# Five plain column pairs instead of six in the first pass, and the second pass's weight sums in its pairs of columns

## The chip, the cores and the metric

The kernel runs on one core of a Trainium2 chip. The metric is the device time of one execution in microseconds (us). TensorE (PE) multiplies matrices, VectorE (DVE), ScalarE (ACT) and GpSimd (POOL) do the element-wise work, SyncE (SP) issues the transfers (DMA). Each engine runs its instructions in the order in which the program has them, and waits on semaphores for the others.

## The reference, cut to what matters

```python
scores = scale * q @ k.T                      # 8 batches, 8 heads, 576 positions, 64 wide
ret = (scores * Dmat) @ v                     # Dmat: gamma ** (i - j) for j <= i, 0 above
x = ret.transpose(0, 2, 1, 3).reshape(4608, 512)
h = x @ w_in                                  # 512 x 2048
g = maximum(h, 0) + log1p(exp(-abs(h)))       # softplus
out = g @ w_out                               # 2048 x 512, float32
```

## The kernel before

Attention has no softmax, so it is done in chunks: within a chunk scores, mask and values, between chunks a state per head. Its output, transposed, is x. The 4608 tokens are 9 units of 512; the two layers then are products of 128x128 weight blocks with 512 tokens. Every float32 operand is split in a high and a low part, and a product of blocks is the three products low x high, high x low and high x high: each is a matmul of 128x128 by 128x512, and a product over two 128-row tiles is 6 of them (`product`). For the second layer `second` does 6 for one block.

Unit 0 opens the kernel alone, while the weights are split. Then units are taken two by two. With two units and two rows and columns of blocks a product needs 8 block products, or 7 in Strassen's (Winograd's) form, with sums of the blocks of weights and of tokens as operands: B11, B21, T1, T2, B22, T3, NT4 name the token sides in the order of use.

- **First pass** (units 1 and 2): the columns of w_in are 8 pairs J. The first `PLAIN` pairs go plain: `plain_slot` is called for 2 x PLAIN columns of unit 1, each with two products, then for as many of unit 2. The other pairs go through `strassen_pair`, 7 products for both units between the two stretches; unit 2's hidden values of these are kept in DRAM and used after its own slots (`kept_parts`). The second layer of these units is plain (`output_some`).
- **Second pass on**: three times `full_pair` for J = 0 to 7 and then `full_phase`, with both layers in the seven-product form.

The weights' sums are made while the first pass runs. `prepare*` makes those of w_in for pair j (4 subtractions or additions on DVE after a sum of the high and low parts, then a split: ACT makes the high part, DVE the low), and stores them as `combined{j}`. `whole_out`, `combine_out`, `split_out` and `store_out` (or `queue_store`) do the same for w_out, as `outcombined{j}`. Before, sums 0 to 4 of w_out are made in the first pass, and 5, 6 and 7 in the first eight `full_pair`s of the second pass, by the table `job(at, ...)`, whose number is the pair J in whose `last_difference` a step stands; `last_difference` runs as `rest[2]` of the next pair.

A ring of 7 buffers feeds the weight blocks: each `product` or `second` takes one, and issues the load of the block seven products later (`block_load`). It then issues one entry of the list `queued`, or two when more than seven are there. All loads and stores go through SP, in program order.

Attention goes on beside this, in groups of some 64 small matmuls: `chunk_products` writes scores and values to the PSUM tiles `two` and `third`. DVE then reads `two` with line 244 (`scores_out`) and line 430 (`halves_out`), and `third` for the states. In a `full_pair` with a group the order on PE is: ..., NT4, the group, the `second` of this pair, then the next pair's B11 (into `acc`) and B21 (into `two[:, 0]`), so B21 has to wait until lines 244 and 430 have read. On DVE, `rest[2:]` and with it the jobs stand in the program ahead of the group's `scores_out`.

Of the kernel before, what the change touches and what calls it, by code (L numbers as in the profile page):

```python
# [52 lines left out]
HI, LO = 0, 1  # L53
TERMS = ((LO, HI), (HI, LO), (HI, HI))
NSUPER = (NUNIT - 1) // 2
PLAIN = 6
RING = 7
QUADS = 9
B11, B22, B21, T1, T3, T2, NT4 = range(7)
# [25 lines left out]
def retention_softplus_ffn(ctx: ExitStack, tc, first, whole, others, consts, w, out):  # L85
# [440 lines left out]
    def output_out(u, tt, last=0):  # L526

        y = ys[u][tt]
        if u not in places:
            places[u] = [quad() for _ in range(2)]  # L530
        osb = places[u][tt // 2][:, tt % 2]
        if tt % 2 == last:
            nc.scalar.copy(osb, y)
        else:
            nc.vector.tensor_copy(osb, y)
        r = u * T + tt * P
        if u < 2:
            nc.sync.dma_start(out[r:r + P, :], osb)
        else:
            behind.append(lambda: nc.sync.dma_start(out[r:r + P, :], osb))  # L540

# [405 lines left out]
    def prepare_sums(j):  # L947
        combine(raws[j])
# [12 lines left out]

    def raw_store(j):
        for p, n in ((2 * j, 2 * P), (2 * j + 1, 4 * P)):
            nc.sync.dma_start(wout_dram[p][:, :, 0:n].bitcast(F32), wouts[p][:, :, 0:n].bitcast(F32))

    def whole_in(j, at):
        whole_out(j, [wout_pools[p].tile([P, 2, T], F32, tag=f"w{p}", name="sums") for p in (2 * at, 2 * at + 1)])
# [23 lines left out]
    def schedule(*rows):  # L991
        plan = {}
        for p, f, *args in rows:
            plan.setdefault(p, []).append(lambda f=f, args=args: f(*args))
        return plan

    def half_b22(i):
# [13 lines left out]
        *[(5 + 2 * j, raw_store, j) for j in range(4)])  # L1011
    starts = schedule(*[(3 + 2 * i, start_combined, i) for i in range(CPU)])
    for p in range(2 * PLAIN):
        group = groups.pop() if p % 2 == 0 and p < 10 else None
        plain_slot(1, p, B11, B21, rest, group, (), *(x.get(p, ()) for x in (jobs, starts)))

    def fetch(J):
# [1 line left out]
        nc.sync.dma_start(g, kept_dram[J])  # L1019
        return g  # L1020

    def strassen_pair(s, J, group, rest, last=False, extra=None):

        u1, u2 = 1 + 2 * s, 2 + 2 * s
        for f in rest[:1]:
# [39 lines left out]
        nc.scalar.copy(c[3], acc)  # L1065
        if extra is not None:
            combine_head(raws["out", extra])
        ab4 = softplus_of(c[3])
        queued_some(len(queued))
        if group:  # L1070
            chunk_products(*group, None)
            coming_steps = next_steps(group[0]) if s == 0 and J == NJ - 1 else []
            group_out(*group)
            if extra is not None:
                combine_rest(raws["out", extra])
            for k in coming_steps:
# [15 lines left out]
    stores = [5]  # L1092
# [7 lines left out]
    extras = {(0, NJ - 2): 1, (0, NJ - 1): 2}  # L1100
    for s in range(FULL):
        u2 = 2 + 2 * s
        first = PLAIN if s == 0 else 0
        more = s + 1 < NSUPER
        for J in range(first, NJ):
            rest, kept = strassen_pair(s, J, groups.pop() if groups else None, rest, s == 0 and J == NJ - 1,
                                       extras.get((s, J)))
        for f in rest:
            f()
        rest = []  # L1110
# [7 lines left out]
        if first:  # L1118
            blocks = schedule((0, prepare_ring, 0))
            plan = schedule(  # L1120
                *[(2 * j - 1, prepare_ring, j) for j in range(1, 4)], *[(2 * j, prepare_sums, j) for j in range(4)],
                *[(2 * j + 1, prepare_split, j) for j in range(4)], *[(2 * j + 2, prepare_store, j) for j in range(4)],
                *[(8 + 2 * i, finish_combined, i, nc.vector) for i in range(2)],
                (9, half_x, B21, STAGE[1, 0], whole, nc.vector), *[(2 * j - 7, raw_store, j) for j in range(4, NJ)],
                (4, whole_in, 3, 0), (6, combine_out, 3), (7, split_out, 3), (8, store_out, 3),
                (8, whole_in, 4, 1), (9, combine_out, 4), (10, split_out, 4), (11, store_out, 4))
            starts = schedule(*[(min(6 + 2 * i, 2 * first - 1), start_combined, i) for i in range(CPU)])
            for p in range(2 * first):
                group = groups.pop() if p % 2 else None
                if p == 0:  # L1130
                    while stores:
                        prepare_rest(stores[0])
                        prepare_store(stores.pop(0))
# [3 lines left out]
                rest = []  # L1137
            job((0, 0), finish_combined, 2, nc.vector)
            job((0, 1), half_x, B11, STAGE[0, 0], whole, nc.vector)
            job((1, 0), finish_combined, 3, nc.vector)  # L1140
            job((1, 1), half_x, B22, STAGE[1, 1], whole, nc.vector)
        else:
            for i in range(CPU):
                job((i + 1, 0), finish_combined, i, nc.vector)
            for n, (b, st) in enumerate(((B11, (0, 0)), (B21, (1, 0)), (B22, (1, 1)))):
                job((5 + n, 0), half_x, b, STAGE[st], whole, nc.vector)
        kept += [fetch(J) for J in range(first + len(kept), first + 2)]
        for n, J in enumerate(range(first, NJ)):
# [2 lines left out]
            kept_parts(u2, J, kept[n], 0)  # L1151
            for f in jobs.get((n, 0), ()):
                f()
            while stores:
                prepare_rest(stores[0])
                prepare_store(stores.pop(0))
# [190 lines left out]
    for s in range(FULL, NSUPER):  # L1347
# [90 lines left out]
```

## Time and profile before

| | us |
|---|---|
| median of 3 runs | 820.41 (820.3 to 820.49) |
| the profiled execution | 820.36 |
| its span on the core | 818.6 |
| TensorE busy | 810.1 |
| VectorE busy | 572.4 |
| ScalarE busy | 394.7 |
| GpSimd busy | 135.4 |

The profile is one execution; the span runs from its first to its last instruction, and 1.76 us of the execution's time lie around it. Busy times are sums over an engine's instructions; engines overlap, so they don't add up to the span.

### The profile page before, as it was taken

To read this page: it belongs to the slowest core of one execution; us is meant where nothing else is said; L and a number is where in the kernel's file an instruction comes from. 1 tells how busy PE (TensorE), PEld (TensorE's weight loads), DVE (VectorE), ACT (ScalarE), POOL (GpSimd) and SP (SyncE) were. 2 spreads that over 40 slices of the span, in tenths; PEclk is the share of its full clock that TensorE was granted. 3 is DMA by queue.
4 is the path that set the end of the run, shared out by engine and by line. 5 is a ranking of instruction groups with operands and counts; after the bars stand their busy time and mean duration, and the time that the engine had idled before them with its cause. 6 is when DMAs were issued, how large, how long until landed. Compare 5 with 4: busy or idle time off the path is not lost.

```text
span 818.6 us, 18782 instructions
## 1 busy us (share of the span) xinstructions
PE 810.1 (99%) x7369; PEld 664.9 (81%) x7369; DVE 572.4 (70%) x962; ACT 394.7 (48%) x698; POOL 135.4 (17%) x208
## 2 busy tenths in 40 slices
PE   8999999999999999999999999999999999999998
PEld 6778878888888888888888888888888888888886
DVE  5999976776676784756869984656769944345785
ACT  6778763324522434534354564334355644434543
POOL 4322221541121453112111000111100000000000
PEclk9999999999999999999999999999999999999999
DMA  9998879887889985698888778778757676666665
GB/s 360 322 314 288 314 241 370 292 293 254 283 307 346 329 281 171 200 318 261 276 260 298 219 222 253 255 234 262 221 170 222 216 242 199 194 195 192 201 212 172
DMA packets 149399, 209.92 MB, mean 256 GB/s; under 512 B 10816, under 2 KB 115008, under 8 KB 149312
## 3 DMA queue, kind: packets, MB, share of 16 engines
q1 hardware_dynamic: 149312, 208.72, 77.4%
q8 instruction: 59, 0.97, 0.5%
q14 instruction: 28, 0.23, 0.1%
HBM read 166.74 MB, written 41.94 MB: 255 GB/s over the span
## 4 chain that ended last, share of the span: by engine, by line
PE 97%; DMA 1%; DVE 0%; SPq 0%; issue 0%; ACT 0%; DVEq 0%
PE acc L891 21%; PE sum L1183 20%; PE y L504 16%; PE third L891 12%; PE h L465 5%; PE two L891 5%; PE two L1183 4%; PE third L226 2%; PE third L1183 2%; PE acc L1183 2%; PE two L210 2%; PE two L288 2%; PE two L300 1%; DMA raw<-whole 1%; PE bank L210 0%
## 5 line engine op out<-in xcount | busy, mean ns | idle before, releaser
L891 PE MATMUL acc<-xt,ring 128*128 128x512 f32 x768 | 193.3, 389 | 0.1
L1183 PE MATMUL sum<-parts,ring 128*128 128x512 f32 (+1 forms) x723 | 173.7, 391 | 0.0
L891 PEld LDWEIGHTS acc<-xt,ring 128*128 128x128 f32 x768 | 143.9, 188 | 30.8 <-DVE quad L1056 0.5
L1183 PEld LDWEIGHTS sum<-parts,ring 128*128 128x128 f32 x723 | 134.2, 188 | 28.2
L1177 DVE TENSOR_TENSOR parts<-g,parts 128x512 fp32r<-128x512 f32 x168 | 113.5, 692 | 52.8 <-ACT parts L1173 51.7
L504 PE MATMUL y<-wout,g 128*128 128x512 f32 x576 | 141.0, 393 | 0.0
L1173 ACT CAST parts<-g 128x512 fp32r<-128x512 f32 x168 | 103.8, 622 | 68.5 <-PE sum L1183 25.3
L504 PEld LDWEIGHTS y<-wout,g 128*128 128x128 f32 x576 | 106.6, 188 | 24.2 <-DVE g L497 1.7
L891 PE MATMUL third<-xt,ring 128*128 128x512 f32 x444 | 110.9, 389 | 0.0
L891 PEld LDWEIGHTS third<-xt,ring 128*128 128x128 f32 x444 | 83.4, 188 | 17.3
L488 ACT ACTIVATE g<-g 128x512 f32<-128x512 f32 x96 | 59.0, 631 | 78.4 <-DVE g L1205 36.2
L203 POOL TENSOR_TENSOR qv<-qv,consts_sb 128x256 f32<-128x256 f32 x61 | 43.0, 705 | 132.8 <-DMA qv<-others 129.3
L1205 DVE TENSOR_TENSOR g<-two,g 128x512 f32<-128x512 f32 x24 | 16.6, 692 | 54.2 <-PE two L891 51.8
L497 DVE TENSOR_TENSOR g<-ab,g 128x512 fp32r<-128x512 f32 x44 | 31.6, 718 | 27.4 <-ACT g L493 26.7
L465 PE MATMUL h<-xt,win 128*128 128x512 f32 x192 | 47.8, 397 | 1.5 <-ACT xt L414 1.5
L493 ACT CAST g<-ab 128x512 fp32r<-128x512 f32 x44 | 27.3, 621 | 44.5 <-PE y L504 40.6
L1203 ACT COPY g<-acc 128x512 f32<-128x512 f32 x24 | 14.1, 588 | 68.7 <-PE acc L891 68.7
L465 PEld LDWEIGHTS h<-xt,win 128*128 128x128 f32 x192 | 35.1, 188 | 10.0 <-ACT xt L414 2.2
L891 PE MATMUL two<-xt,ring 128*128 128x512 f32 x168 | 42.6, 390 | 0.0
L284 POOL TENSOR_TENSOR s<-s,consts_sb 128x256 f32<-128x256 f32 (+1 forms) x31 | 20.7, 667 | 106.7 <-DVE s L282 95.7
L891 PEld LDWEIGHTS two<-xt,ring 128*128 128x128 f32 x168 | 31.4, 188 | 6.8 <-DVE xs L430 0.3
L226 PEld LDWEIGHTS third<-qv,keys 64*64 64x64 f32 x776 | 27.0, 134 | 9.0 <-issue 8.6
(186 smaller groups left out, 1199.7 us busy)
## 6 DMA issues: line engine op xcount, KB each, us to landing
ring<-split SPq DMA_DIRECT2D x126, 256.0 KB, 4.5
ring<-combined SPq DMA_DIRECT2D x104, 256.0 KB, 3.6
ring<-outcombined SPq DMA_DIRECT2D x96, 256.0 KB, 3.4
qv<-others SPq DMA_DIRECT2D x61, 320.0 KB, 4.7
ring<-outsplit SPq DMA_DIRECT2D x72, 256.0 KB, 3.5
wst<-w SPq DMA_DIRECT2D x32, 512.0 KB, 5.8
keys<-others SPq DMA_DIRECT2D x61, 256.0 KB, 4.9
split<-win SPq DMA_DIRECT2D x16, 512.0 KB, 6.0
```

The costliest lines, as they stand in the source:

```text
L203: nc.gpsimd.tensor_mul(v, v, f.unsqueeze(2).broadcast_to([P, 4, D]))
L226: return nc.tensor.matmul(L["T"][rows[h], t, part[s]], L["kp"][rows[t], s, rows[h]], L["v"][rows[t], s, rows[h]], start=True, stop=True, s ...
L284: nc.gpsimd.tensor_mul(s, s, f.unsqueeze(2).broadcast_to([P, 2 * n, D]))
L465: nc.tensor.matmul(h, wins[p][:, a, kt * P:(kt + 1) * P], xt[:, b, T1 + kt // 2, kt % 2], start=(n == 0), stop=(n == 3 * NKT - 1))
L488: nc.scalar.activation(out, h, AF.Softplus)
L493: nc.scalar.copy(g[:, HI], ab)
L497: nc.vector.tensor_sub(g[:, LO], ab, g[:, HI].bitcast(F32))
L504: nc.tensor.matmul(ys[u][tt], g[:, a, tt * P:(tt + 1) * P], wouts[p][:, b], start=(p == 0 and n == 0), stop=(p == NF - 1 and n == 2))
L891: nc.tensor.matmul(bank, w[:, ta, kt * P:(kt + 1) * P], xt[:, tb, x, kt], start=start and k == 0, stop=k == 5, skip_group_check=True)
L1173: nc.scalar.copy(t[:, HI], g_slot(J, n))
L1177: nc.vector.tensor_sub(t[:, LO], g_slot(J, n), t[:, HI].bitcast(F32))
L1183: nc.tensor.matmul(bank[m][:, at], w[:, a, m * P:(m + 1) * P], t[:, b, at], start=start and n == 0, stop=n == 2, skip_group_check=True)
```

## The change

`PLAIN` goes from 6 to 5, so pair 5 of the first pass is a seven-product pair as 6 and 7 are. What the twelfth and eleventh slots did moves: an attention group goes from unit 2's slots to a third `strassen_pair`; the sums of w_in for pair 7 (5, 6 and 7 are needed first now, each before its pair) are made from loads of `split` inside pair 5 by `late_sums`, and sum 4 is made in unit 2's slots, from the ring; the sums 3 and 4 of w_out leave unit 2's slots, and the second pass makes 3, 7, 4, 5 and 6 in that order. `ring_sum`s stand two in a slot instead of four. The stores of units 0 and 1 of the output and those of `raw_store` go through `queued` instead of straight to SP.

```diff
-PLAIN = 6
+PLAIN = 5
...
-        if u < 2:
-            nc.sync.dma_start(out[r:r + P, :], osb)
-        else:
-            behind.append(lambda: nc.sync.dma_start(out[r:r + P, :], osb))
+        (queued if u < 2 else behind).append(lambda: nc.sync.dma_start(out[r:r + P, :], osb))
...
-            nc.sync.dma_start(wout_dram[p][:, :, 0:n].bitcast(F32), wouts[p][:, :, 0:n].bitcast(F32))
+            queued.append(lambda p=p, n=n: nc.sync.dma_start(wout_dram[p][:, :, 0:n].bitcast(F32),
+                                                             wouts[p][:, :, 0:n].bitcast(F32)))
...
-        (6, prepare_ring, 4, 0, 3, 2), (7, prepare_store, PLAIN + 1), (7, prepare_ring, 4, 3, 4, 3),
-        (7, finish_combined, 1, nc.vector), (7, half_b22, 2), (8, prepare_sums, 4), (9, prepare_ring, 5),
-        (9, finish_combined, 2, nc.vector), (10, prepare_split, 4), (10, prepare_sums, 5), (10, half_b22, 3),
-        (11, prepare_store, 4), (11, finish_combined, 3, nc.vector), (11, prepare_head, 5),
+        (7, prepare_store, PLAIN + 1), (7, finish_combined, 1, nc.vector), (7, half_b22, 2), (8, prepare, PLAIN + 2),
+        (9, finish_combined, 2, nc.vector), (9, half_b22, 3), (9, finish_combined, 3, nc.vector),
...
-        for j in stores:
-            prepare_rest(j)
+        if more is not None:
+            prepare_whole(more)
+            prepare_sums(more)
...
+            if more is not None:
+                prepare_rest(more)
+                stores.append(more)
...
-                *[(2 * j - 1, prepare_ring, j) for j in range(1, 4)], *[(2 * j, prepare_sums, j) for j in range(4)],
...
-                (4, whole_in, 3, 0), (6, combine_out, 3), (7, split_out, 3), (8, store_out, 3),
-                (8, whole_in, 4, 1), (9, combine_out, 4), (10, split_out, 4), (11, store_out, 4))
...
+                *[(2 * j - 1, prepare_ring, j, 0, 2) for j in range(1, first)],
+                *[(2 * j, prepare_ring, j, 2, 4) for j in range(1, first)],
...
         if s == FULL:
-            rest = [lambda: None, lambda: None, lambda: whole_in(5, 4), lambda: combine_out(5)]
-            for at, f, *args in ((0, split_out, 5), (0, queue_store, 5), (1, whole_out, 6), (2, combine_out, 6),
-                                 (3, split_out, 6), (3, queue_store, 6),
-                                 (3, lambda: whole_out(7, spare[:2])), (4, combine_out, 7), (5, split_out, 7),
-                                 (5, queue_store, 7)):
-                job(at, f, *args)
+            homes = ((7, lambda: whole_out(7, spare[:2])), (4, lambda: whole_in(4, 7)), (5, lambda: whole_out(5)),
+                     (6, lambda: whole_out(6, spare[:2])))
+            rest = [lambda: None, lambda: None, lambda: whole_out(3), lambda: combine_out(3)]
+            j = 3
+            for at, (following, take) in enumerate(homes):
+                job(at, split_out, j)
+                job(at, queue_store, j)
+                job(at, take)
+                job(at, combine_out, following)
+                j = following
+            job(len(homes), split_out, j)
+            job(len(homes), queue_store, j)
```

Where the second pass's sums stand on DVE is seen in pair 1 of the first eight `full_pair`s. Lines 1274 and 1275 (before) and 1273 and 1274 (changed) are `last_difference`; 673 and 670 are the split's low parts, 652 and 649 `whole_out`, 659 to 662 `combine_out`; 244 and 430 read the attention group's `two`. Before:

```order
L1274 TENSOR_TENSOR g1_4132<-g1_4132 128x512
L1275 TENSOR_TENSOR g1_4132<-g1_4132,g0_4131 128x512 [waits DVE_49]
L673 TENSOR_TENSOR sums_4232<-sums_4232 128x512 [waits Activation_49]
L673 TENSOR_TENSOR sums_4233<-sums_4233 128x512 [waits Activation_49]
L244 TENSOR_TENSOR a_4495<-two_1736,mask_106 128x512 [waits PE_49]
L430 TENSOR_TENSOR xs_595<-two_1736,consts_sb_105 128x4x128
L280 COPY s_4500<-third_1738 128x256 [waits PE_49,Pool_49]
```

With the change, in the same pair:

```order
L1273 TENSOR_TENSOR g1_4109<-g1_4109 128x512
L1274 TENSOR_TENSOR g1_4109<-g1_4109,g0_4108 128x512 [waits DVE_49]
L670 TENSOR_TENSOR quad_4209<-quad_4209 128x512 [waits Activation_49]
L670 TENSOR_TENSOR quad_4210<-quad_4210 128x512 [waits Activation_49]
L649 TENSOR_TENSOR quad_4198<-wout14_979 128x512 [waits DMAHW7_49]
L649 TENSOR_TENSOR quad_4199<-wout15_980 128x512
L659 TENSOR_TENSOR quad_4198<-quad_4198,quad_4199 128x256 [waits DVE_49]
L660 TENSOR_TENSOR quad_4198<-quad_4198 128x256 [waits DVE_49]
L661 TENSOR_TENSOR quad_4199<-quad_4199,quad_4198 128x256 [waits DVE_49]
L662 TENSOR_TENSOR quad_4199<-quad_4198 128x256
L244 TENSOR_TENSOR a_4478<-two_1736,mask_106 128x512 [waits PE_49]
L430 TENSOR_TENSOR xs_595<-two_1736,consts_sb_105 128x4x128
```

Two split operations stood ahead of line 244; now two of the split, two of the next sum's `whole_out` and four of its `combine_out` do. Pairs 2, 3 and 4 have the same eight, for the sums 7 and 4, 4 and 5, 5 and 6. On PE the changed kernel has at the end of pair 1 and the start of pair 2 (the last matmuls of the group, `second`, B11, B21, T2):

```order
L226 MATMUL third_1738<-qv_4328,keys_4339 64x64
L1182 MATMUL sum_4202<-parts_4196,ring_4337 128x512 [waits DMAHW4_49,PE_49,Activation_49]
L1182 MATMUL sum_4202<-parts_4196,ring_4337 128x512 [waits DVE_49]
L1182 MATMUL sum_4202<-parts_4196,ring_4337 128x512
L1182 MATMUL sum_4203<-parts_4196,ring_4337 128x512 x3
L888 MATMUL acc_1737<-xt_186,ring_4348 128x512 [waits DMAHW6_49,Activation_49]
L888 MATMUL acc_1737<-xt_186,ring_4348 128x512 x5
L888 MATMUL two_1736<-xt_186,ring_4364 128x512 [waits DMAHW7_49,DVE_49]
L888 MATMUL two_1736<-xt_186,ring_4364 128x512 x5
L888 MATMUL acc_1737<-xt_186,ring_4374 128x512 [waits DMAHW1_49,Activation_49]
```

This order is the same in both kernels; the matmul into `two` waits for DVE, and what moved is what DVE has to do first. On SP, at the turn from the first seven-product pair of the first pass to the second, the loads for the attention groups stand among the ring's loads. Before (pairs 6 and 7; `keys` and `qv` are the attention's inputs):

```order
L162 DMA keys_2803<-others 128x512 [waits DMAHW1_49,PE_49]
L623 DMA ring_2818<-split0_107 128x2x256 [waits DMAHW2_49,PE_49]
L168 DMA qv_2820<-others 128x640 [waits DMAHW3_49,Pool_49]
L623 DMA ring_2829<-split0_107 128x2x256 [waits DMAHW4_49,PE_49]
L168 DMA qv_2831<-others 128x640 [waits DMAHW5_49,Pool_49]
L623 DMA ring_2853<-split1_108 128x2x256 [waits DMAHW6_49,PE_49]
L162 DMA keys_2855<-others 128x512 [waits DMAHW7_49]
```

With the change, at pairs 5 (the first of three) and 6:

```order
L162 DMA keys_2705<-others 128x512 [waits DMAHW1_49,PE_49]
L620 DMA ring_2720<-split14_121 128x2x256 [waits DMAHW2_49,PE_49]
L168 DMA qv_2722<-others 128x640 [waits DMAHW3_49,Pool_49]
L620 DMA ring_2731<-split14_121 128x2x256 [waits DMAHW4_49,PE_49]
L168 DMA qv_2733<-others 128x640 [waits DMAHW5_49,Pool_49]
L678 DMA combined7_0_137<-quad_2494 128x1024 [waits DMAHW6_49,DVE_49]
L678 DMA combined7_1_138<-quad_2495 128x1024 [waits DMAHW7_49,DVE_49]
L620 DMA ring_2755<-combined7_0_137 128x2x256 [waits DMAHW6_49,DMAHW0_49,PE_49]
L162 DMA keys_2757<-others 128x512 [waits DMAHW1_49]
```

The stores of sum 7 stand now between the `qv` and the `keys` loads of pair 6's group, and the ring load behind them reads back what the first of them stores, so it waits for that store to land.

## Rows read from the trace of the kernel before

**Rows 1.** The page: busy times, busy tenths of TensorE, and the chain that ended last.

```profile
PE 810.1 (99%) x7369; PEld 664.9 (81%) x7369; DVE 572.4 (70%) x962; ACT 394.7 (48%) x698; POOL 135.4 (17%) x208
...
PE   8999999999999999999999999999999999999998
...
PE 97%; DMA 1%; DVE 0%; SPq 0%; issue 0%; ACT 0%; DVEq 0%
```

**Rows 2.** Windows: busy us (instructions) of PE, PEld, DVE, ACT, POOL, clock, DMA.

```profile
460.00:500.00 40.00, 40.00 (x178) 33.11 (x177) 30.71 (x49) 21.83 (x35) 0.00 (x0) 1.00 0.76 229
```

**Rows 3.** Timeline of DVE, second pass, pair 0: start us, us, then the operation.

```profile
332.09 1.29 DVE L652 TENSOR_TENSOR sums<-wout 128x512 f32<-128x512 f32 x2
333.41 0.42 DVE L662 TENSOR_TENSOR sums<-sums 128x256 f32<-128x256 f32 x1
...
335.09 0.68 DVE L244 TENSOR_TENSOR a<-two,mask 128x512 f32<-128x512 f32 x1
335.69 0.68 DVE L430 TENSOR_TENSOR xs<-two,consts_sb 128x512 f32<-128x512 f32 x1
```

**Rows 4.** Timeline of PE, second pass: B21 of pairs 1, 2 and 5.

```profile
336.55 1.32 PE L891 MATMUL two<-xt,ring 128*128 128x512 f32 x5
...
351.03 1.52 PE L891 MATMUL two<-xt,ring 128*128 128x512 f32 x6
...
394.51 1.52 PE L891 MATMUL two<-xt,ring 128*128 128x512 f32 x6
```

**Rows 5.** Timeline of DVE, second pass, pairs 1 and 4.

```profile
346.12 1.29 DVE L673 TENSOR_TENSOR sums<-sums 128x512 fp32r<-128x512 f32 x2
...
389.55 1.28 DVE L673 TENSOR_TENSOR quad<-quad 128x512 fp32r<-128x512 f32 x2
390.76 1.29 DVE L652 TENSOR_TENSOR quad<-wout 128x512 f32<-128x512 f32 x2
391.96 0.69 DVE L244 TENSOR_TENSOR a<-two,mask 128x512 f32<-128x512 f32 x1
```

**Rows 6.** Timeline of DVE, first seven-product pair, the last sum ahead of NT4.

```profile
204.24 0.69 DVE L1056 TENSOR_TENSOR quad<-acc,quad 128x512 f32<-128x512 f32 x1 [1.28 <-PE acc L891]
```

**Rows 7.** Timeline of PE there: output matmuls, NT4, the attention group.

```profile
204.04 0.84 PE L504 MATMUL y<-wout,g 128*128 128x512 f32 x3
204.99 1.66 PE L891 MATMUL acc<-xt,ring 128*128 128x512 f32 x6
206.58 0.73 PE L210 MATMUL two<-qv,keys 64*64 64x64 f32 x21
```

**Rows 8.** Timeline of POOL, second pass, pairs 0 and 1.

```profile
333.93 0.62 POOL L265 COPY sx<-s 64x256 f32<-64x256 f32 x1 [1.34 <-PE third L226]
...
348.42 0.40 POOL L265 COPY sx<-s 64x256 f32<-64x256 f32 x1 [5.29 <-PE third L226]
```

**Rows 9.** Timeline of DVE, last slot of unit 1 and first seven-product pair.

```profile
194.23 1.23 DVE L456 TENSOR_TENSOR xt<-quad,xt 128x1024 fp32r<-128x1024 f32 x1 [0.26 <-ACT xt L455]
...
198.12 1.28 DVE L652 TENSOR_TENSOR quad<-wout 128x512 f32<-128x512 f32 x2
...
202.27 0.69 DVE L1050 TENSOR_TENSOR quad<-third,quad 128x512 f32<-128x512 f32 x1 [1.67 <-PE third L891]
```

**Rows 10.** Timeline of PE: T1 of the first seven-product pair, the second's attention group.

```profile
197.92 1.52 PE L891 MATMUL third<-xt,ring 128*128 128x512 f32 x6
...
223.08 0.27 PE L226 MATMUL third<-qv,keys 64*64 64x64 f32 x1
```

**Rows 11.** Timeline of SP's issues, second seven-product pair.

```profile
213.03 0.55 SPq L168 DMA_DIRECT2D qv<-others  x1
...
215.60 0.59 SPq L162 DMA_DIRECT2D keys<-others  x1
```

**Rows 12.** The page's DMA issues: count, KB each, median us to landing.

```profile
keys<-others SPq DMA_DIRECT2D x61, 256.0 KB, 4.9
...
combined<-quad SPq DMA_DIRECT2D x16, 512.0 KB, 5.3
```

More of the change, by code (lines that the diff above doesn't have):

```diff
@@ L1005, in retention_softplus_ffn @@
         (5, finish_combined, 0, nc.vector), (5, half_b22, 1), (6, prepare_split, PLAIN + 1),
-        (6, prepare_ring, 4, 0, 3, 2), (7, prepare_store, PLAIN + 1), (7, prepare_ring, 4, 3, 4, 3),
-        (7, finish_combined, 1, nc.vector), (7, half_b22, 2), (8, prepare_sums, 4), (9, prepare_ring, 5),
-        (9, finish_combined, 2, nc.vector), (10, prepare_split, 4), (10, prepare_sums, 5), (10, half_b22, 3),
-        (11, prepare_store, 4), (11, finish_combined, 3, nc.vector), (11, prepare_head, 5),
+        (7, prepare_store, PLAIN + 1), (7, finish_combined, 1, nc.vector), (7, half_b22, 2), (8, prepare, PLAIN + 2),
+        (9, finish_combined, 2, nc.vector), (9, half_b22, 3), (9, finish_combined, 3, nc.vector),
         (0, whole_out, 0), (1, combine_out, 0), (2, split_out, 0), (3, store_out, 0),
-        *[(5 + 2 * j, raw_store, j) for j in range(4)])
-    starts = schedule(*[(3 + 2 * i, start_combined, i) for i in range(CPU)])
+        *[(5 + 2 * j, raw_store, j) for j in range(3)])
+    starts = schedule(*[(3 + 2 * i, start_combined, i) for i in range(3)], (8, start_combined, 3, nc.vector))
     for p in range(2 * PLAIN):
-        group = groups.pop() if p % 2 == 0 and p < 10 else None
+        group = groups.pop() if p % 2 == 0 else None
         plain_slot(1, p, B11, B21, rest, group, (), *(x.get(p, ()) for x in (jobs, starts)))
@@ L1020, in fetch, with strassen_pair @@
         return g
-    def strassen_pair(s, J, group, rest, last=False, extra=None):
+    def strassen_pair(s, J, group, rest, last=False, extra=None, more=None):
         u1, u2 = 1 + 2 * s, 2 + 2 * s
@@ L1067, in strassen_pair @@
             combine_head(raws["out", extra])
+        if more is not None:
+            prepare_head(more)
+            if more + 1 < NJ:
+                prepare(more + 1)
         ab4 = softplus_of(c[3])
@@ L1075, in strassen_pair @@
                 combine_rest(raws["out", extra])
+            if more is not None:
+                prepare_rest(more)
+                stores.append(more)
             for k in coming_steps:
@@ L1090, in strassen_pair @@
         return [split_last, lambda: softplus_rest(gs[u1, 2 * J + 1], ab4)], kept
-    stores = [5]
     def kept_parts(u, J, g, n):
@@ L1098, in kept_parts @@
         outputs_of(u, 2 * J + n)
-    extras = {(0, NJ - 2): 1, (0, NJ - 1): 2}
+    stores = []
+    extras = {NJ - 2: 1, NJ - 1: 2}
+    late_sums = {PLAIN: PLAIN + 2}
     for s in range(FULL):
@@ L1106, in retention_softplus_ffn @@
             rest, kept = strassen_pair(s, J, groups.pop() if groups else None, rest, s == 0 and J == NJ - 1,
-                                       extras.get((s, J)))
+                                       extras.get(J), late_sums.get(J))
         for f in rest:
@@ L1120, in retention_softplus_ffn @@
             plan = schedule(
-                *[(2 * j - 1, prepare_ring, j) for j in range(1, 4)], *[(2 * j, prepare_sums, j) for j in range(4)],
-                *[(2 * j + 1, prepare_split, j) for j in range(4)], *[(2 * j + 2, prepare_store, j) for j in range(4)],
-                *[(8 + 2 * i, finish_combined, i, nc.vector) for i in range(2)],
-                (9, half_x, B21, STAGE[1, 0], whole, nc.vector), *[(2 * j - 7, raw_store, j) for j in range(4, NJ)],
-                (4, whole_in, 3, 0), (6, combine_out, 3), (7, split_out, 3), (8, store_out, 3),
-                (8, whole_in, 4, 1), (9, combine_out, 4), (10, split_out, 4), (11, store_out, 4))
-            starts = schedule(*[(min(6 + 2 * i, 2 * first - 1), start_combined, i) for i in range(CPU)])
+                *[(2 * j - 1, prepare_ring, j, 0, 2) for j in range(1, first)],
+                *[(2 * j, prepare_ring, j, 2, 4) for j in range(1, first)],
+                *[(2 * j, prepare_sums, j) for j in range(first)], *[(2 * j + 1, prepare_split, j) for j in range(first)],
+                *[(2 * j + 2, prepare_store, j) for j in range(first - 1)],
+                (6, finish_combined, 0, nc.vector), (8, finish_combined, 1, nc.vector),
+                (9, half_x, B21, STAGE[1, 0], whole, nc.vector),
+                *[(2 * j - 7, raw_store, j) for j in range(4, NJ)], (4, raw_store, 3))
+            starts = schedule(*[(min(4 + 2 * i, 2 * first - 1), start_combined, i) for i in range(CPU)])
             for p in range(2 * first):
                 group = groups.pop() if p % 2 else None
[L1130 to L1133, printed above, removed]
                 if p == 2 * first - 1:
@@ L1137, in retention_softplus_ffn @@
                 rest = []
+            job((0, 0), prepare_store, first - 1)
             job((0, 0), finish_combined, 2, nc.vector)
@@ L1153, in retention_softplus_ffn @@
                 f()
-            while stores:
-                prepare_rest(stores[0])
-                prepare_store(stores.pop(0))
             kept_parts(u2, J, kept[n], 1)
```

## The prediction

> **What bounds it now.** I read the page first: its busy times, its slices and the chain that ended last. TensorE is busy 810.1 of 818.6 us, its tenths are 9 from the second slice to the last but one, and the chain runs through it for 97% of the span [rows 1]. The windows then tell whether "busy" hides a slower clock or gaps: a stretch of the second pass has 178 matmuls in 40.00 us, wholly busy at a granted clock of 1.00, the full 2.4 GHz [rows 2]. That is 0.225 us for each 128x512 matmul, back to back. So DVE's 572 us, ACT's and POOL's cost nothing as long as they are in time. Two kinds of event can move the end: matmuls that go away, and places where TensorE stands because something is late. The slack of such places has to be read from the timelines, DVE against TensorE, and that is where I looked longest.
>
> **What the change removes.** A plain column pair is four slots (two for each unit) of two products, 8; a seven-product pair has 7. The output matmuls are the same for both, and the attention groups are 13 in this stretch before and after, in other places. So one product of 6 matmuls goes: 6 x 0.225 = **1.35 us off** [rows 2]. Nothing else leaves TensorE. As it is full, this is about all that can be gained: the edits that relieve DVE, ACT, POOL or SP gain time only where TensorE stands now, and in the first page's slices it does so at the two ends alone, which the change doesn't touch.
>
> **What it adds: DVE work ahead of a deadline.** The second pass's pairs had one or two steps of a sum each; now pairs 1 to 4 have three: split of one sum, then whole and combine of the next. They stand on DVE ahead of lines 244 and 430, which read the attention group's products from `two`, and the next pair's second product (B21) writes that bank. So it is a race between two engines, and both sides can be read.
>
> DVE's side. The split's two operations take 389.55 to 390.76 = 1.21 us from start to start [rows 5]. The whole takes 332.09 to 333.41 = 1.32, the combine's four 333.41 to 335.09 = 1.68, and lines 244 and 430 335.09 to 336.37 (the second starts at 335.69 and takes 0.68) = 1.28 [rows 3]. Together 5.49 us. The shortest that I can defend takes 1.20 for the whole (390.76 to 391.96, [rows 5]), and 0.22 off the combine, all of what POOL's copy beside it was longer there (0.62 against 0.40, [rows 8]): 5.15.
>
> The start. The jobs begin right behind `last_difference`, whose time follows TensorE's own products and doesn't move with the change: 346.12 in pair 1 and 389.55 in pair 4 [rows 5], pairs 2 and 3 evenly between (14.48 apart). The deadline: B21 of the next pair began at 351.03 and at 394.51 [rows 4], without a gap. Hence 346.12 + 5.49 = 351.61, 0.58 late, and 389.55 + 5.49 = 395.04, 0.53 late; with 5.15 still 0.24 and 0.19. Before, the fullest of these pairs with a split ended its jobs at 391.96 [rows 5] and line 430 some 1.28 later, over a microsecond ahead. And pair 0, which has whole and combine only, has line 430 end at 336.37 against B21 at 336.55: in time by 0.18, which sets how close it can come for free [rows 3, 4]. Pair 5 gets a split and four operations of another kind, under 3 us, and isn't late.
>
> What a late release costs TensorE. The trace has one like it, in the first seven-product pair: the DVE sum ahead of NT4 ended at 204.24 + 0.69 = 204.93 [rows 6]. The three output matmuls from 204.04 should have made room at 204.04 + 3 x 0.225 = 204.71, but NT4 began at 204.99, and its six matmuls took until 206.58, 1.59 instead of 1.35 [rows 7]. So the loss is the lateness plus 0.06 at least, plus 0.30 at most (part of the 0.24 is the change to small matmuls). With pair 0's free 0.18 in mind I take the lateness plus 0.17: 0.55 + 0.17, about 0.70 for each pair. **Four pairs: 2.8 us added**; bounds 4 x (0.2 + 0.06) = 1.0 and 4 x (0.58 + 0.30) = 3.5. The delay isn't regained, as TensorE has no slack, and it doesn't grow from pair to pair, as the next pair's DVE work is released by products that are late by the same amount.
>
> **What I cost at nothing**, with the cover.
> - Sum 7 of w_in inside pair 5: whole 1.3 and combine 1.7 on DVE where the first seven-product pair had a whole and a split from 198.12; the next operation that TensorE waits for came at 202.27 [rows 9]. 198.12 + 3.0 = 201.1 fits; with it gone, up to 0.7 us.
> - The last slot of unit 1 now makes two parts of the combined tokens instead of one: another 1.23 and a smaller one behind 194.23 + 1.23 [rows 9], some 197.0, and T1 needs them at 197.92 [rows 10]. The tightest of these: 0.9 us left.
> - The sums that leave unit 2's slots, and ring sums two by two: DVE has less to do there. Stores through `queued`: SP's waits for them come later, and the ring's loads are issued seven products ahead. The plain slots lose cover nowhere that I find.
> - The wait at NT4 (lateness 0.22, loss about 0.4) is that of the first seven-product pair, and goes with it from pair 6 to pair 5.
>
> **A rule that speaks against it.** POOL's copy of the states falls among these jobs: in pair 1 at 348.42 [rows 8], while by the sum the whole is just ending and the combine begins. In pair 0 such an overlap lengthened the copy by 0.22, and the 1.68 that I use has in it what DVE lost. *The Trainium skill, page "SBUF — State Buffer", section "Who interferes with whom", says that a DVE instruction with two SBUF inputs contends with a GpSimd instruction that reads SBUF, the one that is second being fully blocked until the other has ended. Row and rule agree on the contention; only the rule would make DVE wait a whole copy.* By the row the sum stays; with DVE blocked for a whole copy, 0.40 us [rows 8], in each of four pairs, it is 1.6 more: a rival below.
>
> **Sum**, against the profiled execution's 820.36 us (span 818.6 and 1.76 around it; the median is 820.41): 820.36 - 1.35 + 2.8 = **821.8 us**, bounds 820.36 - 1.35 + 1.0 = 820.0 and 822.5. About 0.2%, 1.64 us, is what a measurement can tell from no change here: faster begins below 818.77, slower above 822.05.
>
> **The rivals.**
> - *The jobs fit.* DVE would have to be 0.5 us quicker in each pair than the rows, or the wait be placed otherwise. For it: less work of other kinds between, and the order is only the program's. Against it: every duration comes from the same operations on the same sizes, and the changed order shows the wait on DVE at B21. Then only the product counts: 819.0. 12%.
> - *A load for attention is late* (the slower side by itself). Before, SP issued the second `keys` load of the second seven-product pair's group at 215.60 [rows 11]; the group began at 223.08 [rows 10], 7.5 us later, and a `keys` load lands in 4.9 [rows 12]: 2.6 us spare. Now two stores of sum 7 stand after the `qv` load (213.03 + 0.55 = 213.6, [rows 11]) and a ring load that reads the first of them back stands ahead of the `keys` load. The store lands at 213.6 + 5.3 = 218.9 by the median [rows 12], the two issues take some 1.2 more, so `keys` lands near 220.1 + 4.9 = 225.0 by medians, 1.9 late; a store and a load that land 1 us quicker each, as half of them do by some amount, make it nothing. It decides once store and load take over 8.3 us together. Medians hold for half of the cases, so I take a loss of 0.5 to 1.3 as this rival's, added to the main sum: 822.3 to 823.1, middle 822.7. 18%.
> - *DVE blocked by POOL* for whole copies, as above: 821.8 + 1.6 = 823.4. It needs POOL to hold the port at the start of a DVE operation in every pair. 7%.
> - *More is freed than a product*: the waits at NT4 vanish because the pair that comes first has another neighbour, and the jobs fit as well: 820.36 - 1.35 - 0.4, 818.6 or less. 8%.
>
> **How the numbers follow.** The forecast, four short waits at B21, has 55%, with its own range 820.0 to 822.5. Of this 55, 38 lie within 0.2% and 17 above it. Faster: the last rival, 0.08. Same: 0.38 + 0.12 = 0.50. Slower: 0.17 + 0.18 + 0.07 = 0.42. The range leaves out the last rival and most of POOL's, and reaches a little below the case in which the jobs fit: 818.8 to 823.3.
>
> **What would show it.** In the second pass's pairs 1 to 4 a gap of 0.6 to 0.8 us on TensorE between B11 and B21, put down to DVE line 430, and none in pairs 0 and 5; DVE without idle time from `last_difference` to line 430 there. Six matmuls of 128x512 fewer. No gap in the last slot of unit 1 or at T1 of pair 5. If the group of pair 6 begins late and waits for `keys`, the second rival holds. My forecast is wrong if B21 shows no gaps, if these are over 1 us each, or if TensorE stands somewhere in the first pass for over half a microsecond.

## The result, and the profile after

The changed kernel takes 826.0 us (median of 6 runs, 823.93 to 827.8) against 820.36 us (6 runs, 820.17 to 820.7): ratio 1.0067, 95% interval 1.0057 to 1.0077. It is slower by 5.6 us, and its runs lie 3.9 us apart where those of before lie 0.5 apart. Later runs of the kernel before, 11 to 23 beside the experiments, lay 1.6 to 2.5 us apart but for one execution of 2926 us, so the 0.5 is no measure of its scatter. The profiled execution took 825.75 us, 5.39 more than that of before.

The page's busy times and chain, which answer to [rows 1]:

```profile
PE 811.4 (98%) x7363; PEld 664.3 (81%) x7363; DVE 573.7 (70%) x967; ACT 397.1 (48%) x701; POOL 130.2 (16%) x205
...
PE 89%; DVE 5%; DMA 2%; issue 1%; POOL 1%; ACT 1%; SPq 0%; DVEq 0%; POOLq 0%; ACTq 0%
```

TensorE has six matmuls fewer, as forecast. But the chain, 97% TensorE before, now goes through DVE, DMA, POOL and ACT as well: TensorE stands, and in more than one kind of place. The waits of TensorE (engine, line, what it waited for: us in total, times, longest):

```profile
PE two L888 <- DVE xs L430: 1.7, 4, 0.5
...
PE two L300 <- issue: 1.3, 1, 1.3
...
PE third L888 <- DVE s L282: 1.0, 1, 1.0
PE y L504 <- DVE g L497: 0.5, 1, 0.5
```

The waits for fill, xt and raw between these rows are those of the opening. The first row is the forecast; the other three weren't in it. Two of them, at 287 and 314 us, stand in the first pass, and a loss of over half a microsecond there was the prediction's own sign of being wrong.

**The four waits at B21.** DVE and then TensorE, pair 1 of the second pass, to be read beside [rows 4, 5]:

```profile
348.92 1.29 DVE L670 TENSOR_TENSOR quad<-quad 128x512 fp32r<-128x512 f32 x2
350.12 1.29 DVE L649 TENSOR_TENSOR quad<-wout 128x512 f32<-128x512 f32 x2
351.44 0.50 DVE L659 TENSOR_TENSOR quad<-quad 128x256 f32<-128x256 f32 x1
...
353.12 0.68 DVE L244 TENSOR_TENSOR a<-two,mask 128x512 f32<-128x512 f32 x1
353.72 0.68 DVE L430 TENSOR_TENSOR xs<-two,consts_sb 128x512 f32<-128x512 f32 x1
```

```profile
352.70 1.29 PE L888 MATMUL acc<-xt,ring 128*128 128x512 f32 x5
354.45 1.43 PE L888 MATMUL two<-xt,ring 128*128 128x512 f32 x5 [0.46 <-DVE xs L430]
```

DVE works without a break from 348.92 to 354.40, 5.48 us. The five matmuls shown of B11, its last five of six, end their turn at 352.70 + 5 x 0.227 = 353.83, and B21 starts at 354.45: 0.62 lost, and another 0.11 between its first two matmuls. The four gaps are 0.62, 0.59, 0.58 and 0.58, with 0.11 behind each: 2.8 us.

**Unit 2's slot 6.** DVE, then POOL, then TensorE:

```profile
280.27 1.83 DVE L643 TENSOR_TENSOR quad<-ring 128x256 f32<-128x256 f32 x2
282.13 0.84 DVE L659 TENSOR_TENSOR quad<-quad 128x256 f32<-128x256 f32 x1
...
284.63 1.21 DVE L456 TENSOR_TENSOR xt<-quad,xt 128x1024 fp32r<-128x1024 f32 x1
...
286.66 0.42 DVE L282 TENSOR_TENSOR s<-third,u 128x256 f32<-128x256 f32 x1
```

```profile
279.76 1.19 POOL L448 TENSOR_TENSOR quad<-xs 128x256 f32<-128x256 f32 x1
...
282.65 0.91 POOL L451 TENSOR_TENSOR quad<-xs,quad 128x256 f32<-128x256 f32 x1
```

```profile
287.14 1.20 PE L888 MATMUL third<-xt,ring 128*128 128x512 f32 x4 [0.95 <-DVE s L282]
```

Two ring sums (line 643), the combine and a part of the combined tokens (456) stand in this slot, and POOL's start of the next part (448 to 451) runs beside them. The last two came here by lines of the change that the diff above leaves out: with two slots fewer, DVE's line 456 for parts 0 and 1 went from slots 8 and 10 to 6 and 8, and POOL's starts from slots 6, 8, 10 and 11 to 4, 6, 8 and 9. A ring sum takes 0.92 and the combine's first operation 0.84, where an operation of that size took 0.42 in [rows 3]. The state that the next slot's bank `third` waits for (line 282) is late, and TensorE loses 1.1 us and 0.1 behind it.

**The kept pairs.** The chain of waits there, in order of time (start, us, what):

```profile
297.89 5.98 DMA qv<-others
...
303.94 1.16 POOL qv L203
...
306.12 1.69 POOL quad L448
...
310.63 1.16 POOL quad L451
...
311.81 1.06 ACT xt L455
...
312.89 1.23 DVE xt L456
314.12 0.61 DVE g L497
...
314.77 1.45 PE y L504 x5
```

POOL has the last start of combined tokens (448 to 451) behind the scaling of `qv`, whose load lands at 303.87. ACT's cast (455) waits for POOL's last operation and DVE's line 456 for that cast. Behind these two, in the program order of ACT and DVE, stand the hidden values (497) that the output matmuls need: 0.7 us lost, and 0.1 behind it.

**Pair 0's attention group.** TensorE in the middle of the group's small matmuls:

```profile
334.69 0.22 PE L300 MATMUL two<-qv,s 64*64 64x64 f32 x1
336.21 0.27 PE L300 MATMUL two<-qv,s 64*64 64x64 f32 x1 [1.30 <-issue]
```

No semaphore stands there; "issue" is time in which the engine waited for nothing that the profile shows. The DMA queues show something. In the changed kernel from 325 to 332 us (packets, MB, share), and from 332 to 336:

```profile
q1 hardware_dynamic: 772, 0.74, 36.5%
```

```profile
q1 hardware_dynamic: 289, 0.30, 28.5%
q8 instruction: 1, 0.02, 1.6%
```

In the kernel before, from 325 to 332:

```profile
q1 hardware_dynamic: 522, 0.50, 21.8%
q8 instruction: 1, 0.02, 1.0%
```

A 16 KB piece of TensorE's instructions (queue q8 brings 59 in the whole run; 7363 matmuls and as many weight loads make some 250 for each) came in ahead of the group before (which began at 331.67 and ended at 333.8; the next piece came at 334.5), and during the group now, from 333.73 to 334.75. The group needs some 256 instructions in 1.9 us. So it looked like a shortage of instructions, and it was worth testing.

Summed up: -1.36 + 2.8 + 1.2 + 0.8 + 1.5 = 4.9 of the 5.39 us.

### The profile page after: what moved, and what is told of

The parts are those of the page before. It is cut to its first block, busy times and chain, and to the rows that moved or that the text cites. A ratio compares the mean times of both kernels' runs of the same rounds, so it can differ in the third digit from the quotient of the medians.

```text
span 824.0 us, 18781 instructions
## 1 busy us (share of the span) xinstructions
PE 811.4 (98%) x7363; PEld 664.3 (81%) x7363; DVE 573.7 (70%) x967; ACT 397.1 (48%) x701; POOL 130.2 (16%) x205
## 4 chain that ended last, share of the span: by engine, by line
PE 89%; DVE 5%; DMA 2%; issue 1%; POOL 1%; ACT 1%; SPq 0%; DVEq 0%; POOLq 0%; ACTq 0%
PE acc L888 19%; PE sum L1182 19%; PE y L504 14%; PE third L888 12%; PE h L465 5%; PE two L888 5%; PE two L1182 4%; PE third L1182 2%; PE acc L1182 2%; PE third L226 2%; PE two L288 1%; PE two L210 1%; DMA raw<-whole 1%; PE two L300 1%; DMA qv<-others 1%
## 5 line engine op out<-in xcount | busy, mean ns | idle before, releaser
L888 PE MATMUL third<-xt,ring 128*128 128x512 f32 x432 | 108.3, 389 | 1.0 <-DVE s L282 1.0
L888 PEld LDWEIGHTS third<-xt,ring 128*128 128x128 f32 x432 | 81.0, 188 | 18.2 <-DVE s L282 1.4
L203 POOL TENSOR_TENSOR qv<-qv,consts_sb 128x256 f32<-128x256 f32 x61 | 45.1, 739 | 129.1 <-DMA qv<-others 125.2
L888 PE MATMUL two<-xt,ring 128*128 128x512 f32 x174 | 44.7, 393 | 1.7 <-DVE xs L430 1.7
```

Of the source, the lines that this page charges most:

```text
L203: nc.gpsimd.tensor_mul(v, v, f.unsqueeze(2).broadcast_to([P, 4, D]))
L888: nc.tensor.matmul(bank, w[:, ta, kt * P:(kt + 1) * P], xt[:, tb, x, kt], start=start and k == 0, stop=k == 5, skip_group_check=True)
```

## The experiments

Times are medians against the kernel before on the same chip in the same session, whose median was 820.65 to 820.75 us. The changed kernel wasn't run again beside them, so a gain over its 826.0 us compares two sessions and is less sure than the gaps in the traces.

**e1_fills.** The shortage of instructions, by moving everything in the stream:

```diff
-FILLS = 22
+FILLS = 86
```

> The changed kernel with 64 more tiny matmuls in the opening, where TensorE waits for loads anyway: nothing is computed otherwise, but every later instruction of TensorE stands 128 places further on in its instruction stream. Theory (the 1.3 us in pair 0's attention group in which TensorE waited for nothing the profile shows are a shortage of instructions, set by where the stream's 16 KB pieces end): the gap at about 334.9 us is gone or stands elsewhere, time about 824.5 us if it is gone. Rival (the gap belongs to something in that group, such as an operand or the quiet queue ahead of it): the gap stays where it is, 826 us.

831.94 us, ratio 1.013 (1.0117 to 1.0143): a miss as to the time. The gap in pair 0's group is gone, but the opening has a worse one of the same kind (waits of TensorE):

```profile
PE pair L360 <- issue: 3.4, 1, 3.4
```

A piece came in from 9.88 to 10.82 us, and TensorE went on at 12.25; from 10 to 20 us the granted clock was 0.83 on average.

The expectation also had the shift wrong: each fill is two matmuls in the trace, so 64 of them with their weight loads are 256 instructions, just one piece, and the trace has 60 pieces instead of 59. The group stood where it had stood within a piece, and yet had no gap: its piece began at 334.54, 4.0 us ahead of it. So this run shows that instructions can be short elsewhere too; that the place within a piece decides, it doesn't show.

**e2_ring.** Ring sums four to a slot again:

```diff
-                *[(2 * j - 1, prepare_ring, j, 0, 2) for j in range(1, first)],
-                *[(2 * j, prepare_ring, j, 2, 4) for j in range(1, first)],
+                *[(2 * j - 1, prepare_ring, j) for j in range(1, first)],
```

> The changed kernel with the ring sums of unit 2's slots back four to a slot, in the odd slots, as before. Theory (two ring sums of 0.95 us each in slot 6, doubled by GpSimd's work beside them, make VectorE late for the state that slot 7's third bank waits for): the wait of 1.0 us of the third bank for line 282 goes, 826.0 - 1.2 = 824.8 us. Rival (slot 6 is too full anyway through the earlier finish of the combined tokens, or the odd slots become late instead): a wait of 0.5 us or more stays there or shows in slot 5 or 7, time within 0.5 us of the changed kernel.

825.82 us, 1.0057 (1.0036 to 1.0078), runs from 823.1 to 829.33. Of the gap ahead of `third` 0.3 of 1.1 us is left, so that step held; the time hardly shows it. In the profiled run the gap in pair 0's group was 2.05 us, and this followed (windows: busy us and instructions of PE, PEld, DVE, ACT, POOL, then clock, DMA share and GB/s; and one row of TensorE's timeline):

```profile
336.00:340.00 4.00, 4.00 (x17) 3.12 (x11) 2.46 (x5) 0.00 (x0) 1.01 (x2) 0.57 0.00 0
```

```profile
336.06 2.68 PE L1181 MATMUL sum<-parts,ring 128*128 128x512 f32 x6
```

The granted clock was 0.57 on average over these 4 us, and matmuls came 0.43 us apart instead of 0.227: the lower level of 1.2 GHz for eight matmuls, 1.6 us more. After the gap of 1.30 us in the changed kernel's profile the clock stayed at 1.00, as it did after gaps of 1.43 to 1.50 in e4, e5 and f2 below.

**e3_finish.** The last part of the combined tokens later:

```diff
-            job((1, 0), finish_combined, 3, nc.vector)
+            job((2, 0), finish_combined, 3, nc.vector)
```

> The changed kernel with the last part of the combined tokens finished one kept pair later. Theory (its cast waits for GpSimd's last subtraction and holds up the hidden values' split behind it on ScalarE and VectorE): the wait of the output matmuls for line 497 at about 314 us goes, 826.0 - 0.8 = 825.2 us. Rival (the wait moves to the second pass's first products, which read these tokens): a gap of half a microsecond or more in pair 0, no gain.

825.28 us, 1.0052 (1.004 to 1.0065). The wait at 314 us is gone and nothing is late in pair 0; one of 0.4 us for line 497 shows at 305 instead. The profiled run again had a long gap in pair 0's group, 1.76 us, and the slow stretch behind it (a granted clock of 0.66 from 336 to 341 us).

**e4_spread.** The second pass's sums cut finer (the combine in halves of two operations):

```diff
+            for at, f, *args in ((0, split_out, 3), (0, queue_store, 3), (0, lambda: whole_out(7, spare[:2])),
+                                 (0, combine_half, 7, 0),
+                                 (1, combine_half, 7, 1), (1, lambda: whole_in(4, 7)), (1, combine_half, 4, 0),
...
+                                 (5, combine_half, 6, 1), (5, split_out, 6), (5, queue_store, 6)):
+                job(at, f, *args)
...
-                job(4 + i, start, i)
+                job(4 + i if s > FULL else divmod(9 + 2 * i, NJ), start, i)
```

> The changed kernel with the second pass's weight sums cut finer: no pair has more than about 3.3 us of them ahead of line 244, the sum for pair 6 ends one pair later, and the two starts of combined tokens stand in the phase that follows. Theory (B21 waits because eight operations take 5.5 us where 4.9 are to be had): all four gaps at B21 go, 826.0 - 2.8 = 823.2 us. Rival (the gaps only move, to the phase's start, where the last sum's load or the moved starts are late): less than 1.4 us gained, and a gap of over 1 us after pair 7.

824.53 us, 1.0046 (1.0034 to 1.0058): about 1.5 below the changed kernel's median instead of 2.8. All four gaps at B21 are gone, and B21 follows B11 at once:

```profile
354.14 1.52 PE L900 MATMUL acc<-xt,ring 128*128 128x512 f32 x6
355.50 1.52 PE L900 MATMUL two<-xt,ring 128*128 128x512 f32 x6
```

In the phase two gaps of 0.42 us have come up where DVE's split is late, behind the moved starts, and the wait for line 497 in the kept pairs was 0.9 us in this profile. So the theory's step held and its time didn't; a part of the rival's came as well.

**f1_after24 and f2_before20.** The place in the stream from both sides. Counted in the program (a matmul and its weight load one instruction each, a semaphore wait one), pair 0's group begins at place 7124 before and at 7119 after the change. Two fills are 8 places.

```diff
-FILLS = 22
+FILLS = 24
```

> The changed kernel with two more tiny matmuls in the opening: the attention group of pair 0 in the second pass stands 8 instructions further on in TensorE's stream, 3 beyond where it stood before the change (the change had moved it 5 back). Theory A (the gap in that group comes about when a 16 KB piece of the stream is asked for only after the group's first instruction, which waits; 5 places decide it): no gap there, 826.0 - 1.5 to 3.5, about 823.5 us, and runs closer together. Theory B (the timing of the quiet stretch ahead of the group decides, not the place in the stream): the gap stays, about 826 us with the same scatter.

824.56 us, 1.0046 (1.0034 to 1.0058), five runs from 824.11 to 825.04. The gap is gone, and the piece comes ahead of the group (325 to 332 us):

```profile
q1 hardware_dynamic: 731, 0.70, 31.7%
q8 instruction: 1, 0.02, 0.9%
```

The kernel before with

```diff
-FILLS = 22
+FILLS = 20
```

> The kernel before with two tiny matmuls fewer in the opening: the same attention group stands 8 instructions earlier, 3 ahead of where the changed kernel has it. Theory A: a gap of 1 to 2 us opens in that group though nothing else is changed, 822 to 824 us with a scatter. Theory B: no gap, 820.4 us.

822.79 us, 1.002 (1.0008 to 1.0032), twelve runs from 820.28 to 824.84. Its profile has the gap, in the same group, in a kernel that is otherwise the one before:

```profile
337.96 0.21 PE L226 MATMUL third<-qv,keys 64*64 64x64 f32 x1 [1.50 <-issue]
```

The forecast of theory A for the gap held both ways. The times are less clear: of the 4.5 us by which f2's profiled execution is longer than that of before, 1.9 are in this group, while 2.1 were lost ahead of 121 us. And with the gap 5 to 12 runs of a kernel lie 2.3 to 6.2 us apart (the changed kernel, e2 to e5, f2), without it 5 to 23 runs 0.5 to 2.5 (f1, c1 to c4, the kernel before).

All 13 traces, counted in the same way, agree but for e1. The six with the group at place 7116 or 7119 (the changed kernel, e2 to e5, f2) have the gap; the six at 7124 or 7127 (the kernel before, f1, c1 to c4) don't; nor does e1 at 7375, 256 places behind 7119. In the six with the gap the piece's transfer begins 0.9 to 1.7 us after the group's first matmul, and TensorE goes on 1.4 to 1.6 us after the transfer has ended. In the other seven it begins 4 to 7 us ahead of the group.

**e5_pool.** POOL's start out of slot 6:

```diff
-            starts = schedule(*[(min(4 + 2 * i, 2 * first - 1), start_combined, i) for i in range(CPU)])
+            starts = schedule(*[((4, 7, 8, 9)[i], start_combined, i) for i in range(CPU)])
```

> The changed kernel with GpSimd's second start of combined tokens one slot later, in slot 7 of unit 2 instead of slot 6; VectorE's work in slot 6 stays as it is. Theory (VectorE's operations with two SBUF operands take twice as long beside GpSimd's, and only so is slot 6 too full): the ring sums and the combine in slot 6 take 0.42 us each and the third bank's wait for line 282 is gone, 1.2 us less if nothing else moves. Rival (slot 6 has too many operations whatever runs beside them): the wait stays above 0.5 us.

826.05 us, 1.0065 (1.0053 to 1.0077). DVE in slot 6, the same operations as above:

```profile
279.60 0.75 DVE L643 TENSOR_TENSOR quad<-ring 128x256 f32<-128x256 f32 x2
280.38 0.43 DVE L659 TENSOR_TENSOR quad<-quad 128x256 f32<-128x256 f32 x1
```

0.75 for two instead of 1.83 and 0.43 instead of 0.84, and the wait for line 282 is gone: the theory's mechanism held. No time is gained, since the later start makes another thing late: ACT's cast of that part waits for POOL until 295.8, and behind it a copy that the next attention group needs (waits of TensorE):

```profile
PE third L226 <- ACT mark L348: 1.9, 1, 1.9
```

**c1_best, c2_best, c3_nospread, c4_best.** All repairs together. c1 has e2's and e4's edits (with one start in the last pair), two more fills, and the kept pairs as

```diff
+            job((0, 1), finish_combined, 2, nc.vector)
+            job((1, 0), half_x, B11, STAGE[0, 0], whole, nc.vector)
+            job((1, 1), finish_combined, 3, nc.vector)
+            job((2, 0), half_x, B22, STAGE[1, 1], whole, nc.vector)
```

> The changed kernel with all that the first experiments point to: ring sums four to a slot as before, the parts of the combined tokens finished half a kept pair later each, the second pass's sums cut finer with one start of combined tokens in the last pair and one in the phase, and two more tiny matmuls in the opening. Theory (the waits add up and have these four causes): nothing left but the product saved and some tenths of waits, 819.0 to 820.0 us, ahead of the kernel before by 0.5 to 1.4 us. Rival (the waits come back in other places, as VectorE, ScalarE and GpSimd have the same work in shorter stretches): 821 us or more.

820.79 us, 0.9999 (0.999 to 1.0007): 5 us back, but not ahead. Left were 0.7 us where the start made line 430 late for the phase's first bank, and 0.8 us in the attention group of pair 6 of the first pass. c2 has the starts at `(0, 3)` and `(0, 5)` and

```diff
-                stores.append(more)
+                prepare_store(more)
```

> The version with all repairs again, with two things changed that its profile showed: both starts of combined tokens in the phase, at its fourth and sixth block, where VectorE has room, and sum 7's store of the first pass issued as soon as it is made, ahead of the loads for the next pair's attention group. Theory (what was left were line 244 late behind the start in the last pair, 0.7 us, and the group of pair 6 waiting for keys, 0.3 to 0.8): 819.2 us, faster than before by 0.1 to 0.2%. Rival (a few tenths turn up wherever work is put): 820.3 us or more, no difference to before.

820.51 us, 0.9997 (0.9987 to 1.0006): the rival's number. Both waits were gone; there were gaps of 0.2 and 0.4 us in the phase, where the starts now stand, and one of 0.3 in unit 2's slot 7. c3 is c2 with the second pass's sums as the change has them.

> The same, but with the second pass's sums as the change has them. Theory (the four waits at B21 cost 0.7 us each whatever goes on ahead of them): 2.8 us more than the run beside it, about 822.0 us. Rival (part of that was due to the late start of the second pass): under 2 us more.

822.08 us, 1.0017 (1.0008 to 1.0026), 1.57 more than c2, which is the rival's number again. Its four gaps at B21 are 0.61, 0.59, 0.58 and 0.58, just those of the changed kernel. TensorE comes to the last `second` of the eight pairs (c2, then c3)

```profile
434.62 1.66 PE L1193 MATMUL sum<-parts,ring 128*128 128x512 f32 x6
```

```profile
437.68 1.66 PE L1181 MATMUL sum<-parts,ring 128*128 128x512 f32 x6
```

3.06 us later, of which 0.14 were there when pair 0's group began. So the four gaps cost 2.9 us whatever goes on ahead of them, as the theory has it. In the phase that follows c2 then loses 1.2 of its lead to its own gaps there, and so the times are closer. c4 cuts the starts:

```diff
+                    for n, at in enumerate(((2, 3, 4, 5), (6, 7, 9, 11))[i]):
+                        job(divmod(at, NJ), start_part, i, n)
...
-                (6, finish_combined, 0, nc.vector), (8, finish_combined, 1, nc.vector),
+                (7, finish_combined, 0, nc.vector), (8, finish_combined, 1, nc.vector),
```

> The repaired version once more, with the two starts of combined tokens cut into their four operations each, one to a block of the phase, and the first part of the combined tokens finished in slot 7 of unit 2 instead of slot 6. Theory (the two gaps of 0.2 and 0.4 us in the phase and the 0.3 us at unit 2's slot 7 come from work in one piece that fits when it is cut): none of the three left, 819.4 us, faster than before by 0.1 to 0.2%. Rival (what is left is in the opening and in run-to-run scatter): 820.2 us or more.

819.97 us (12 runs, 818.65 to 820.65), 0.9991 (0.9982 to 0.9999): ahead of the kernel before by 0.7 us, with an interval of 0.1 to 1.5, between what theory and rival said. All waits of TensorE that its profile lists:

```profile
PE idle L712 <- DVE fill L695: 1.5, 1, 1.5
PE h L465 <- ACT xt L414: 1.5, 2, 1.1
PE y L504 <- issue: 0.7, 1, 0.7
PE pair L360 <- DMA raw<-whole: 0.4, 1, 0.4
```

But for one of 0.7 us, only the opening's are left. That one stands among plain output matmuls:

```profile
299.95 1.31 PE L504 MATMUL y<-wout,g 128*128 128x512 f32 x5 [0.71 <-issue]
```

A piece of instructions came in from 297.68 to 298.56, and TensorE went on 1.4 us after that, as in pair 0's group. No run tests it by itself.

## Why the prediction was wrong

- **The product saved**, 1.35 us: right. Six matmuls fewer, and c4, which has nearly all waits out, shows half of it as time, within an interval that reaches from nearly nothing to all of it.
- **Four waits at B21**, 2.8 us: right in place, count and size (0.62 to 0.58, and 0.11 behind each; forecast 0.70 each). DVE's jobs took 5.48 us against 5.49, and in pair 1 their start and TensorE's deadline both came 2.80 us later than before, as the reasoning needs. e4 takes the gaps away, c3 has them with all else repaired. That DVE would wait for whole copies of POOL, the rival at 7%, didn't come about.
- **The step that failed** is the list of what was costed at nothing, and in it the sentence "The plain slots lose cover nowhere that I find". It compared DVE's sum of work over unit 2's slots, which fell, and not the slots one by one, and it has no entry for POOL's starts and DVE's line 456, which moved two slots earlier. Slot 6 has two ring sums, a combine, a part of the tokens and POOL's start together: 1.2 us. In the kept pairs POOL's last start became the end of a chain: 0.8 us. e5 takes the first of these waits away and e2 most of it, e3 the second. With these two and the 1.5 us below, 821.8 becomes 825.3, against the profiled 825.75.
- **The port between DVE and POOL** was looked for in the second pass only, where it cost nothing beyond the forecast. It cost time in unit 2's slots: with POOL beside it DVE took 0.83 to 0.92 for what takes 0.42, and e5 shows this by moving POOL alone. The Trainium skill, page "SBUF — State Buffer", section "Who interferes with whom", states that a DVE instruction with two inputs in SBUF contends with a GpSimd instruction that reads SBUF; these rows agree.
- **Nothing in the sum allowed for the supply of instructions.** It was put at nothing without being named, and made 1.5 us in the profiled run. f1 and f2 show the gap go and come with 8 places in the stream. The Trainium skill, page "Runtime: NRT & Kernel Launch", section "Instruction fetch mechanics", has the next 16 KB fetched while the current ones run, mostly hidden; here 1.3 to 2.1 us weren't. That the spread of the changed kernel's runs, 823.9 to 827.8, comes from this gap is supported by f1's narrow spread, but not shown. The slow clock isn't its cause: the mean granted clock is on record for every run, and is 1.0 in five of the six, the fastest and the slowest among them, and 0.999 in the profiled one, where e2's and e3's profiled runs with the slow stretch have 0.998 and 0.997.
- **The rival of the late load** had its place right: pair 6's group stood for 0.26 us in the middle of its matmuls, and c2, which issues the store earlier, has no gap there, where c1 had 0.8. c2's other edit stands in the second pass, some 220 us later, so the gap there goes with the store. The loss was less than the 0.5 to 1.3 us that the rival had.

What stays open is what decides when a piece of instructions is asked for. e1 had the group at the same place within a piece as the changed kernel, and its piece came in time. Some 0.5 of the 5.39 us are accounted for only in part, by the 0.26 in pair 6's group.

## What to carry to other kernels

When work on a side engine moves, lay it out slot by slot against each deadline, with the engine that shares its port beside it; a sum over a stretch that falls says nothing of the fullest slot. When TensorE has no slack, every burst of small matmuls needs its instructions in time: after an edit that changes their number, look for waits put down to "issue" within such a burst, and try a few instructions more or less ahead of it. A repair of one wait should be read in the trace, not in the time, as long as another one scatters by more.

## What the runs showed of the hardware that was not expected

A burst of some 256 small instructions of TensorE in 1.9 us ran dry for 1.3 to 2.1 us when its 16 KB piece came in during the burst, and went on 1.4 to 1.6 us after the transfer of the piece had ended (six runs). After such a pause of 2.05 us the granted clock stood at the lower level for eight matmuls (0.43 us each instead of 0.227), and it fell after one of 1.76 us too; after those of 1.30 to 1.50 us it didn't. DVE's 128x256 operations on two SBUF operands took 0.83 to 0.92 us beside POOL's and 0.42 alone.
